# Load order of keys, queries and values, and two FFN matmuls moved ahead of a granule's transposes, in a one-core attention and FFN kernel

## The chip, the cores and the metric

The kernel runs on one core of one Trainium2 chip. The metric is device time in microseconds (us); a smaller time is better. Times inside a profile count from the start of its span, which is about 1.7 us shorter than the device time.

## The reference

Windowed attention with eight global keys feeds a feed-forward network (FFN) with a squared ReLU. There are 4 batches, 8 heads, 768 positions and a head size of 64; the FFN is 512 to 2048 to 512.

```
scores = q @ k.T / sqrt(D) - slope[h] * dist        # only global keys and the last 96 positions are kept
a      = softmax(scores)
x      = (a @ v), heads side by side                # 3072 x 512
out    = (s * relu(x @ w_in)**2 + b) @ w_out        # 3072 x 512
```

## The kernel before

The sequence is worked in twelve *granules* of 256 rows, numbered 0 to 11 in the code. The text below says third granule for `j == 2`, fifth for `j == 4`, and so on. A granule has two *blocks* of 128 rows. From the third granule on, the keys, queries and values of a granule come as six loads of 128 KB (counted as written), all issued by GpSimd (the first two granules are loaded by other lines of the code):

```
def load_granule(j):
    b, g = divmod(j, NGR)
    t = nat_tile(j)
    for i in range(GB):                  # two blocks
        sb = g * GB + i
        for n in range(2):               # keys, then queries
            nc.gpsimd.dma_start(t[:, n, i, :, :], rows_of(srcs[n], b, sb))
        nc.gpsimd.dma_start(vbuf[b % 2][:, sb, :, 0:D], rows_of(v, b, sb))
```

Keys and queries must be transposed before the scores. For the first four granules TensorE (PE) does it, through PSUM; from the fifth on it is done by DMA transposes that SyncE issues:

```
def qk_wide(j, n, evac):                 # PE: 8 transposes, then one evacuation
    ps = ps_h.tile([P, GB, HP, P], BF16, name="ps_t", tag="psh")
    for i in range(GB):
        for hp in range(HP):
            nc.tensor.transpose(ps[:, i, hp, :], nat[j][:, n, i, 2*hp : 2*hp+2, :], ident_bf[:])
    evac(qk_of(b, n)[:, g * GB : (g + 1) * GB], ps[:])

def qk_by_dma(j):                        # SyncE: key, query of block 0, then of block 1
    for i in range(GB):
        for n in range(2):
            nc.sync.dma_start_transpose(qk_of(b, n)[:, g * GB + i], ...)
```

The main body is a hand-made schedule. With cuts:

```
    load_granule(2)
    load_granule(3)
    ...
    load_granule(4)
    load_granule(5)
    ...
    p2_mm(0, 1, lo, FC)                  # second FFN product of the first granule
    p2_hold(0, 1)                        # ScalarE empties its PSUM buffer

    qk_wide(2, 0, nc.vector.tensor_copy) # third granule: keys
    qk_wide(2, 1, nc.scalar.copy)        #                queries
    make_koff(2)                         # shifted keys, VectorE
    make_voff(2)                         # shifted values, VectorE
    p2_mm(1, 0, 0, FC // 2)              # 8 matmuls of 128x512
    e8, m8, e9, m9 = scores(4)           # first scores of the third granule
    ...
    qk_by_dma(4)                         # fifth granule: keys and queries, by DMA
    ...
    finish_granule(3)
    run(scores(8))                       # first scores of the fifth granule
    make_voff(4)
    p2_mm(2, 0, 0, FC // 2)
```

## Time and profile before

| | before |
|---|---|
| device time, median of 3 runs | 209.34 us (209.31 to 209.69) |
| span in the profile | 207.7 us |
| PE busy | 97% of the span |
| third granule: transposes start, first scores start | 38.12, 41.70 us |
| fifth granule: first scores start, FFN matmuls behind them start | 60.02, 60.72 us |

The page of the kernel before, its first lines and its chain by line. The chain is followed back from the last instruction, and a share is that of the span.

```profile
span 207.7 us, 5321 instructions
PE 202.2 (97%) x2191; PEld 160.2 (77%) x2191; DVE 159.5 (77%) x336; ACT 128.7 (62%) x200; POOL 70.4 (34%) x90
...
PE 82%; DMA 15%; ACT 1%; DVE 1%; issue 0%; POOL 0%
```

PE is the limit for most of the span: it is hardly ever idle, and the chain is PE for 82% of it. The place where the chain is a DMA comes from the chain of waits in order of time (start, duration, what):

```profile
13.33 13.78 DMA w_out_bf<-in_moe_w_out_dram
27.11 0.28 issue
27.39 12.21 DMA nat<-in_q_dram
39.60 0.05 issue
39.65 0.40 PE ps_t L350 x4
40.04 1.73 PE ps L666 x8
```

The load of the third granule's second query block lands at 39.60 us, and PE waits for it. PE's own timeline there (start, duration, engine, line, operation, output and inputs, shapes, count, and in brackets the idle time before and what ended it) shows the same hole from the other side:

```profile
38.12 0.39 PE L350 MATMUL ps_t<-ident_bf,nat 128*128 128x128 bf16 x4
38.84 0.62 PE L350 MATMUL ps_t<-ident_bf,nat 128*128 128x128 bf16 x8 [0.34 <-DMA nat<-in_k_dram]
39.65 0.40 PE L350 MATMUL ps_t<-ident_bf,nat 128*128 128x128 bf16 x4 [0.18 <-DMA nat<-in_q_dram]
39.88 1.89 PE L666 MATMUL ps<-w_out_bf,gT 128*128 128x512 bf16 x8
41.70 0.40 PE L440 MATMUL ps_s<-qx,kx 64*128 64x128 bf16 x8
```

Sixteen transposes stand in three pieces with waits between. The FFN matmuls behind them needed nothing that was late, but stood behind the waiting transposes in program order.

These are the first scores of the fifth granule, in the same timeline:

```profile
60.02 0.55 PE L440 MATMUL ps_s<-qx,kx 64*128 64x128 bf16 x8
60.38 0.40 PE L440 MATMUL ps_s<-qx,ko 64*128 64x128 bf16 x8
60.72 1.04 PE L666 MATMUL ps<-w_out_bf,gT 128*128 128x512 bf16 x4
```

The same eight score matmuls take 0.40 us at 41.70 us and 0.55 us here. No wait is named, because the idle time is hidden inside the merged line. The single records of the trace show where it is: the first two of these matmuls start at 60.02 us, the third at 60.22 us. The first two need block 0 of the granule, the third needs block 1. It is a wait of about 0.15 us for something that had only just arrived, and the result turns on it.

### The profile page before, as it was taken

The page shows a single profiled execution, that of the slowest core. Times are in us where ns is not written, and L with a number is a line of the kernel's source. Part 1 is how long each engine was busy: PE and PEld are TensorE (multiplying, and loading weights), DVE is VectorE, ACT ScalarE, POOL GpSimd, SP SyncE. Part 2 cuts the span into 40 slices and gives each one's busy share as a digit, 9 for nine tenths or more (in the row PEclk, how much of TensorE's full clock was granted, in tenths as well). Part 3 has the DMA queues.
Part 4 walks back from the last instruction along what each step waited for, and adds up shares of the span by engine and source line. Part 5 has one row for each costly group of instructions (what it writes and reads, how often), then busy time and mean ns, then how long its engine had stood idle before and what let it go on. Part 6 is the DMA issues. An engine that isn't in the chain of part 4 may idle for free.

```text
span 207.7 us, 5321 instructions
## 1 busy us (share of the span) xinstructions
PE 202.2 (97%) x2191; PEld 160.2 (77%) x2191; DVE 159.5 (77%) x336; ACT 128.7 (62%) x200; POOL 70.4 (34%) x90
## 2 busy tenths in 40 slices
PE   7999999899999999999999999999999999999993
PEld 2678884456876685778888898888898889888883
DVE  7586599858989955799799974699865696737974
ACT  4975669485975648786564495664695764476200
POOL 8995334899726202805501906400000000000000
PEclk9999999999999999999999999999999999999999
DMA  5999999999999999999999999995460300240006
GB/s 162 173 179 202 207 207 177 155 152 136 116 149 135 155 156 197 147 234 205 143 230 140 113 124 201 183 204 69 52 205 3 88 17 0 53 153 0 0 7 198
DMA packets 110836, 28.17 MB, mean 136 GB/s; under 512 B 97852, under 2 KB 109308, under 8 KB 110812
## 3 DMA queue, kind: packets, MB, share of 16 engines
q0 software_dynamic: 76000, 13.11, 87.8%
q1 hardware_dynamic: 33612, 14.13, 36.8%
q10 hardware_dynamic: 1200, 0.59, 1.1%
q8 instruction: 17, 0.28, 0.6%
q14 instruction: 7, 0.06, 0.1%
HBM read 27.26 MB, written 6.29 MB: 162 GB/s over the span
## 4 chain that ended last, share of the span: by engine, by line
PE 82%; DMA 15%; ACT 1%; DVE 1%; issue 0%; POOL 0%
PE ps L618 34%; PE ps L818 24%; PE ps L666 10%; DMA w_out_bf<-in_moe_w_out_dram 7%; DMA nat<-in_q_dram 6%; PE ps_s L440 6%; PE ps_av L494 5%; DMA first<-in_q_dram 2%; PE ps_t L350 1%; ACT qx L330 1%; PE ps_last L818 0%; PE ps_x L590 0%; ACT open_bf L231 0%; ACT nat L259 0%; PE ps_t L340 0%
## 5 line engine op out<-in xcount | busy, mean ns | idle before, releaser
L618 PE MATMUL ps<-xT,w_in_bf 128*128 128x256 bf16 x768 | 90.3, 273 | 0.0
L628 ACT ACTIVATE gT<-ps 128x512 bf16<-128x512 f32 x96 | 55.8, 598 | 46.8 <-PE ps L618 46.5
L618 PEld LDWEIGHTS <-w_in_bf 128*128 128x128 bf16 x768 | 73.0, 98 | 9.4 <-DVE xT L593 0.2
L449 ACT ACTIVATE pt<-ps_s 128x1024 bf16<-128x1024 f32 (+1 forms) x44 | 39.3, 945 | 3.2 <-PE ps_s L440 3.2
L666 PE MATMUL ps<-w_out_bf,gT 128*128 128x512 bf16 x128 | 29.7, 380 | 0.0
L456 DVE TENSOR_TENSOR pt<-pt,tmpl 128x1024 bf16<-128x1024 bf16 (+1 forms) x40 | 24.6, 646 | 4.6 <-ACT pt L449 4.5
L818 PEld LDWEIGHTS <-gsum 128*128 128x128 bf16 x256 | 24.1, 98 | 3.7 <-DVE gsum L781 0.5
L792 DVE TENSOR_TENSOR gT<-gT 128x1024 bf16<-128x1024 bf16 x20 | 13.7, 687 | 11.7 <-ACT gT L628 11.7
L666 PEld LDWEIGHTS <-gT 128*128 128x128 bf16 x128 | 11.7, 98 | 13.0
L465 DVE TENSOR_TENSOR xn<-ps_av,rc 128x256 bf16<-128x256 f32 x48 | 20.4, 425 | 1.7
L818 PEld LDWEIGHTS <-gT 128*128 128x128 bf16 x200 | 18.6, 98 | 2.3
L116 POOL DMA_DIRECT2D nat<-in_k_dram x20 | 18.1, 903 | 6.2 <-issue 1.8
L116 POOL DMA_DIRECT2D nat<-in_q_dram x20 | 18.0, 902 | 5.9 <-DMA w_out_bf<-in_moe_w_out_dram 3.4
L117 POOL DMA_DIRECT2D vb<-in_v_dram x20 | 18.0, 900 | 5.9 <-DMA w_in_bf<-in_moe_w_in_dram 2.0
L464 DVE RECIPROCAL rc<-ps_av 128x4 f32<-128x4 f32 x48 | 8.6, 179 | 12.2 <-PE ps_av L494 10.3
L494 PEld LDWEIGHTS <-pt 128*128 128x128 bf16 x320 | 14.4, 97 | 2.7 <-DVE xn L465 0.7
L631 DVE TENSOR_TENSOR gT<-gT 128x512 bf16<-128x512 bf16 x32 | 13.0, 422 | 3.7 <-ACT gT L628 3.3
L122 POOL COPY gate<-xT 1x1 bf16<-1x1 bf16 x6 | 1.9, 323 | 41.0 <-DMA xT<-xn 38.9
L494 PE MATMUL ps_av<-vb,pt 128*128 128x65 bf16 x208 | 15.4, 193 | 0.0
L818 PE MATMUL ps<-w_out_bf,gsum 128*128 128x256 bf16 x128 | 15.3, 273 | 0.0
L818 PE MATMUL ps<-wsub,gsum 128*128 128x256 bf16 x128 | 15.1, 273 | 0.0
L818 PE MATMUL ps<-w_out_bf,gT 128*128 128x256 bf16 x120 | 13.9, 273 | 0.0
(112 smaller groups left out, 223.7 us busy)
## 6 DMA issues: line engine op xcount, KB each, us to landing
out_dram<-o_q SPq DMA_DIRECT2D x15, 256.0 KB, 2.5
vb<-in_v_dram POOLq DMA_DIRECT2D x24, 128.0 KB, 7.3
nat<-in_k_dram POOLq DMA_DIRECT2D x22, 128.0 KB, 6.8
nat<-in_q_dram POOLq DMA_DIRECT2D x22, 128.0 KB, 7.0
w_out_bf<-in_moe_w_out_dram POOLq DMA_DIRECT2D x4, 512.0 KB, 16.2
w_in_bf<-in_moe_w_in_dram POOLq DMA_DIRECT2D x4, 256.0 KB, 7.4
w_in_bf<-in_moe_w_in_dram POOLq DMA_DIRECT2D x2, 512.0 KB, 11.3
out_dram<-o_sb SPq DMA_DIRECT2D x4, 256.0 KB, 5.9
```

What stands on the lines that cost most here:

```text
L116: nc.gpsimd.dma_start(t[:, n, i, :, :], rows_of(srcs[n], b, sb))
L117: nc.gpsimd.dma_start(vbuf[b % 2][:, sb, :, 0:D], rows_of(v, b, sb))
L449: nc.scalar.activation(pt[:, :, 0:ncol], ps[:, :, 0:ncol], ACT.Exp, scale=QSCALE)
L456: nc.vector.tensor_tensor(pv, pv, m.rearrange("p h a c -> p h (a c)"), ALU.mult)
L465: nc.vector.tensor_tensor(dst, av[:, :, :, 0:D], rc[:].to_broadcast((P, 2, 2, D)), ALU.mult)
L494: nc.tensor.matmul(av[:, i, hi, 0 : D + 1], lhsT=pt[:, hi, c * P : (c + 1) * P], rhs=vv, start=(n == 0), stop=(n == len(terms) - 1),)
L618: nc.tensor.matmul(ps[:, i, :], lhsT=w_in_bf[:, kc, fc * P : (fc + 1) * P], rhs=xT[j][:, kc, :], start=(kc == 0), stop=(kc == KC - 1),)
L628: nc.scalar.activation(gs, ps[:], ACT.Relu)
L631: nc.vector.tensor_tensor(gs, gs, gs, ALU.mult)
L666: nc.tensor.matmul(po[:], lhsT=g_of(j)[:, fc, tb * P : (tb + 1) * P], rhs=w_out_bf[:, fc, :], start=(fc == 0), stop=(fc == FC - 1),)
L792: outs.append(lambda: nc.vector.tensor_tensor(gs, gs, gs, ALU.mult))
L818: nc.tensor.matmul(ps[:, tb, cs], lhsT=stat[:, fc, tb * P : (tb + 1) * P], rhs=mov[:, fc, cs], start=(fc == 0), stop=(fc == NH - 1),)
```

## The change

Its intent is to close the hole at the third granule, in two ways. Keys and queries of both blocks are loaded ahead of both value blocks, in every granule from the third on, so the second query block lands one load sooner. Two FFN matmuls that are ready go in front of the transposes, so PE has work while the last loads land.

```
@@ load_granule
             for n in range(2):
                 nc.gpsimd.dma_start(t[:, n, i, :, :], rows_of(srcs[n], b, sb))
-            nc.gpsimd.dma_start(vbuf[b % 2][:, sb, :, 0:D], rows_of(v, b, sb))
+        load_v(j)

@@ main body
+    p2_mm(1, 0, 0, 2)
     qk_wide(2, 0, nc.vector.tensor_copy)
     qk_wide(2, 1, nc.scalar.copy)
     make_koff(2)
     make_voff(2)
-    p2_mm(1, 0, 0, FC // 2)
+    p2_mm(1, 0, 2, FC // 2)
```

More of the change, by code (lines that the diff above doesn't have):

```diff
@@ L116, in load_granule @@
                 nc.gpsimd.dma_start(t[:, n, i, :, :], rows_of(srcs[n], b, sb))
-            nc.gpsimd.dma_start(vbuf[b % 2][:, sb, :, 0:D], rows_of(v, b, sb))
+        load_v(j)
     def hold_loads(ap):
@@ L1088 @@
     p2_hold(0, 1)
+    p2_mm(1, 0, 0, 2)
     qk_wide(2, 0, nc.vector.tensor_copy)
@@ L1094 @@
     make_voff(2)
-    p2_mm(1, 0, 0, FC // 2)
+    p2_mm(1, 0, 2, FC // 2)
     e8, m8, e9, m9 = scores(4)
```

## The prediction

> **What bounds the kernel now.** TensorE. The page gives PE 97% busy at full granted clock. The chain of waits, in order of time, is nothing but matmuls from 39.6 us to 203 us, so what makes PE get there earlier shortens the whole as much, unless another wait opens. The chain before it is a DMA stretch: from 13.3 us it follows the second-FFN weights, then the load of the third granule's queries, issued at 27.39 us and landing 12.21 us later, at 39.60 us. The timeline of PE shows the hole: the third granule's 16 transposes start at 38.12 us, the second key block's wait (0.34 us idle), the last query block's wait (0.18 us idle) and the FFN matmuls behind them start at 40.04 us. Elsewhere in the chain eight such transposes take 0.45 us, so sixteen 0.90; here they take 1.92. The hole is worth about 1.0 us.
>
> **What the change does.** It adds and removes no work.
>
> 1. Load order. The packets of the load queue in the trace show it streaming back to back, about 0.86 us for each 128 KB load. Estimated landings before: k0 36.2, q0 37.0, v0 37.85, k1 38.75, q1 39.6, v1 40.45 us. Moving v0 behind q1 puts k1 near 37.9 and q1 near 38.7; v0 goes to 39.6; v1 stays.
> 2. Two FFN matmuls (0.43 us; eight take 1.73) go in front of the transposes. They are ready at 38.12 us. The Trainium skill, "TensorE: Matmul & The Clock Gate", Part 2, says that matmuls stay in program order and only weight loads are pulled ahead; the trace agrees, since ready FFN matmuls sat behind the waiting transposes until 40.04 us. They also cover a second wait: in the changed kernel the query transposes use the PSUM buffer that ScalarE empties at 38.91 us.
>
> Estimated order after: two matmuls 38.12 to 38.55, key transposes to 39.0, query transposes to 39.45, six matmuls to 40.75, then the scores, which began at 41.70 us before. That is about 1.0 us sooner.
>
> **What could take some back.** Six matmuls instead of eight now cover the evacuations. Query copy on ScalarE: 1.01 us from about 39.65, done near 40.7, needed at 40.75. Key copy and shifted-key copies on VectorE: 1.74 us from about 39.2, done near 40.95, needed at 41.0. Both just fit; I allow 0 to 0.2 us of new waits. The shifted values need v0 at about 40.5 us, and it is there at 39.6. The first value product of this granule moves to 43.7 us, with v1 landed at 40.45. Later granules load well ahead of use.
>
> **Predicted time.** 209.34 minus about 0.95 = 208.4 us, range 208.0 to 209.0. Chances: faster by over 2%: 0.01; within 2%: 0.98; slower by over 2%: 0.01.
>
> **What would show it right or wrong.** Right: in PE's timeline no idle time at the third granule's transposes; the 16 of them in about 0.9 us; the scores of that granule beginning near 40.75 us; all later pieces of the chain shifted by 0.9 to 1.0 us. Load step wrong: the transposes still wait for a DMA. Matmul step wrong: the two matmuls wait for ScalarE. Give-back: scores waiting for the query copy on ScalarE or the shifted-key copy on VectorE.
>
> **What would make it wrong.** The weights landing later in the changed run, moving everything; a new wait of the scores larger than 0.2 us; a later place where PE waits for a fixed DMA time, so that the lead is lost again; the masks being held behind the value copy on VectorE.

## The result, and the profile after

| | before | after |
|---|---|---|
| device time, median of 4 runs each | 209.51 us (209.31 to 209.69) | 209.27 us (209.03 to 209.31) |
| ratio, 95% interval | | 0.9986 (0.9969 to 1.0004) |
| span in the profile | 207.7 us | 207.3 us |
| third granule: first scores start | 41.70 us | 40.89 us |
| fifth granule: first scores start | 60.02 us | 59.20 us |
| fifth granule: FFN matmuls behind them start | 60.72 us | 60.31 us |

A ratio is the mean time of one kernel's runs over that of the other's of the same rounds, so it is not quite the ratio of the medians quoted. The gain is 0.24 us by the medians, 0.1% of the time, and the interval of the ratio includes no gain at all. About 0.95 us was predicted.

PE's timeline after the change, at the third granule:

```profile
38.60 1.06 PE L350 MATMUL ps_t<-ident_bf,nat 128*128 128x128 bf16 x16
39.49 1.46 PE L666 MATMUL ps<-w_out_bf,gT 128*128 128x512 bf16 x5
40.89 0.40 PE L440 MATMUL ps_s<-qx,kx 64*128 64x128 bf16 x8
```

The hole is closed: the sixteen transposes are one piece with no wait, and the scores start 0.81 us sooner (41.70 to 40.89). (Five FFN matmuls are recorded where the program has six; some matmul records are missing from a trace.) The same timeline at the fifth granule:

```profile
58.66 0.61 PE L590 MATMUL ps_x<-ident_bf,xn 128*128 128x128 bf16 x8
59.20 0.23 PE L440 MATMUL ps_s<-qx,kx 64*128 64x128 bf16 x2
59.81 0.34 PE L440 MATMUL ps_s<-qx,kx 64*128 64x128 bf16 x6 [0.39 <-DMA qx<-nat]
59.98 0.40 PE L440 MATMUL ps_s<-qx,ko 64*128 64x128 bf16 x8
60.31 1.47 PE L666 MATMUL ps<-w_out_bf,gT 128*128 128x512 bf16 x5
```

PE brings the lead undiminished for 18 us: it reaches these scores at 59.20 us and not at 60.02. Two matmuls run, and then it waits, for the DMA transpose of the queries. Past the scores the lead is 0.41 us (60.72 to 60.31). The page's chain by engine has moved accordingly, with less PE and more DMA in it:

```profile
span 207.3 us, 5315 instructions
...
PE 69%; DMA 19%; POOL 6%; SPq 2%; issue 1%; DVE 0%; POOLq 0%
```

and the chain of waits in order of time now runs through this DMA:

```profile
52.10 7.67 DMA qx<-nat
59.77 0.04 issue
59.81 0.57 PE ps_s L440 x14
```

SyncE's timeline shows the four DMA transposes of the fifth granule in the kernel before:

```profile
46.85 1.31 SPq L359 DMA_TRANSPOSE kx<-nat  x1
51.02 1.75 SPq L359 DMA_TRANSPOSE qx<-nat  x1
```

and after (first and fourth only, in both):

```profile
47.08 1.29 SPq L359 DMA_TRANSPOSE kx<-nat  x1
52.10 1.27 SPq L359 DMA_TRANSPOSE qx<-nat  x1
```

The first of them is issued when the fifth granule's first keys have landed, and PE's lead does not make that sooner: 46.85 us before, 47.08 us after. The packet records of the trace (each transpose moves 512 packets of 256 bytes on SyncE's queue) give the last data packet of the fourth transpose: 59.49 us before, 59.08 us after. PE goes on 0.7 us after that packet, at 60.22 us before and 59.81 us after (up to 1.0 us in the runs below), so a last packet that comes a little ahead of PE's arrival still makes it wait. Both kernels run into the same landing there, the kernel before by about 0.15 us and the changed one by 0.39 us.

### The profile page after: what moved, and what is told of

Same layout as the page of the kernel before. It is cut to its first block, busy times and chain, and to the rows that moved or that the text cites. A ratio compares the mean times of both kernels' runs of the same rounds, so it can differ in the third digit from the quotient of the medians. Undisturbed runs are those within 1.5% of the kernel's fastest.

```text
span 207.3 us, 5315 instructions
## 1 busy us (share of the span) xinstructions
PE 201.4 (97%) x2183; PEld 160.2 (77%) x2191; DVE 159.8 (77%) x336; ACT 128.7 (62%) x200; POOL 69.3 (33%) x90
## 4 chain that ended last, share of the span: by engine, by line
PE 69%; DMA 19%; POOL 6%; SPq 2%; issue 1%; DVE 0%; POOLq 0%
PE ps L618 31%; PE ps L818 24%; DMA w_out_bf<-in_moe_w_out_dram 8%; PE ps L666 7%; PE ps_s L440 4%; DMA vb<-in_v_dram 4%; DMA qx<-nat 4%; PE ps_av L494 4%; DMA nat<-in_k_dram 3%; SPq L359 2%; POOL vb L108 2%; POOL nat L102 2%; POOL nat L116 1%; POOL w_in_bf L140 1%; PE ps_last L818 0%
## 5 line engine op out<-in xcount | busy, mean ns | idle before, releaser
L666 PE MATMUL ps<-w_out_bf,gT 128*128 128x512 bf16 x120 | 28.7, 380 | 0.5 <-issue 0.2
L108 POOL DMA_DIRECT2D vb<-in_v_dram x24 | 21.4, 905 | 7.8 <-DMA w_out_bf<-in_moe_w_out_dram 3.4
L122 POOL COPY gate<-xT 1x1 bf16<-1x1 bf16 x6 | 1.1, 176 | 40.4 <-DMA xT<-xn 38.0
```

The source lines that it names most:

```text
L666: nc.tensor.matmul(po[:], lhsT=g_of(j)[:, fc, tb * P : (tb + 1) * P], rhs=w_out_bf[:, fc, :], start=(fc == 0), stop=(fc == FC - 1),)
```

## The experiments

The theory: two limits stand in series. One is the hole at the third granule. The other is the landing of the fifth granule's DMA-transposed queries near 60 us, which PE does not set. The change removes the first, and its lead is given back at the second. The rivals: A, nothing is lost later and the gain was over-sized; B, the new load order itself delays the fifth granule; D, raised later, an early load alone makes the gain.

The table gathers what the runs showed. "Arrives" is the first score matmul of the fifth granule, "last packet" the last data packet of its fourth DMA transpose, "leaves" the start of the FFN matmuls behind these scores, all in us from the profile. The last column works from the ratio, as (ratio - 1) times the median of before in the same rounds. That median was 209.30 us in one set of rounds and 209.69 us in another on the same chip, so times of different rounds are not to be compared directly.

| run | arrives | last packet | PE's named wait | leaves | median | before | gain by ratio |
|---|---|---|---|---|---|---|---|
| before | 60.02 | 59.49 | none | 60.72 | 209.51 | | |
| after | 59.20 | 59.08 | 0.39 | 60.31 | 209.27 | 209.51 | -0.29 |
| e1 loads only | 59.43 | 59.85 | 0.90 | 61.06 | 209.69 | 209.51 | -0.13 |
| e2 matmuls only | 59.53 | 59.31 | 0.39 | 60.66 | 209.16 | 209.51 | -0.31 |
| e3 both, fifth early | 59.13 | 57.59 | none | 59.69 | 208.58 | 209.51 | -0.98 |
| e4 both, fill | 60.21 | 59.85 | none | 61.04 | 209.16 | 209.51 | -0.40 |
| e5 neither, fifth early | 60.05 | 57.99 | none | 60.60 | 209.29 | 209.30 | -0.06 |
| e6 matmuls, fifth early | 59.59 | 57.68 | none | 60.22 | 209.03 | 209.30 | -0.31 |
| e7 loads, fifth early | 59.50 | 57.72 | none | 60.06 | 208.66 | 209.30 | -0.75 |
| e8 both, sixth held | 59.23 | 56.42 | none | 59.78 | 208.77 | 209.30 | -0.54 |
| e9 both, again | 59.27 | 59.87 | 1.39 | 61.39 | 209.67 | 209.69 | +0.13 |
| e10 both, fifth early, again | 59.22 | 57.75 | none | 59.87 | 208.69 | 209.69 | -0.88 |
| e11 the same and a fill | 59.60 | 57.93 | none | 60.15 | 209.16 | 209.69 | -0.57 |

In e4 two of the FFN matmuls stand in front of the scores, so its "arrives" and "leaves" are not those of the others.

The profiles also show that little else counts in these executions. One granule later, at the start of the FFN matmuls behind the sixth granule's first scores (near 70 us), the lead or lag against the kernel before is the difference in the whole span to within 0.05 us in ten of the twelve profiles (after: 0.40 and 0.39 us ahead; e1: 0.34 and 0.34 behind; e7: 0.66 and 0.67 ahead; e9: 0.67 and 0.63 behind). The two others lose something later: e3 0.11 us and e11 0.42 us.

### Each part of the change alone (e1, e2)

The first keeps the change's load order and puts the two matmuls back:

```
-    p2_mm(1, 0, 0, 2)
     qk_wide(2, 0, nc.vector.tensor_copy)
...
-    p2_mm(1, 0, 2, FC // 2)
+    p2_mm(1, 0, 0, FC // 2)
```

> Only the load order of the change; the two FFN matmuls stay where they were. Theory (the lead made at the third granule, 38 to 41 us, is given back at the first scores of the fifth granule, near 59.8 us, because the DMA transposes of its queries land at a time that PE does not set): lead of about 0.5 us over the kernel before at the third granule's first scores, and 0.3 to 0.4 us left after the fifth granule's first scores; time about 0.3 us under before, the same as the full change. Rival A (nothing is lost later, the gain was over-sized): the same lead at 41 us and at 61 us, and a time under before by just that lead. Rival B (the new load order delays the fifth granule's loads and causes the loss): the loss is here in full, so the same times as the theory.

The second is the opposite: the kernel before, with the two matmuls moved and the load order left alone.

> Only the two FFN matmuls ahead of the third granule's transposes; load order as before. Theory: lead of about 0.4 us at the third granule's first scores; the transposes of the fifth granule's queries land where they did before (PE held until about 60.2 us), so at most 0.2 us is left after those scores, and the time is 0 to 0.2 us under before. Rival B (the load order causes the loss): the 0.4 us lead is kept to the end, time 0.4 us under before. Rival A: also 0.4 us kept.

Both parts do what they should at the third granule. Its first scores start at 41.12 us with the loads alone and at 41.22 us with the matmuls alone, leads of 0.58 and 0.48 us. Both lose at the fifth granule. PE's timeline of e1 there:

```profile
59.43 0.23 PE L440 MATMUL ps_s<-qx,kx 64*128 64x128 bf16 x2
60.56 0.34 PE L440 MATMUL ps_s<-qx,kx 64*128 64x128 bf16 x6 [0.90 <-DMA qx<-nat]
60.73 0.40 PE L440 MATMUL ps_s<-qx,ko 64*128 64x128 bf16 x8
61.06 0.82 PE L666 MATMUL ps<-w_out_bf,gT 128*128 128x512 bf16 x2
```

In this execution e1 comes out 0.34 us *behind* the kernel before (61.06 against 60.72), although it arrived 0.59 us ahead. PE's timeline of e2 has the same wait:

```profile
60.16 0.34 PE L440 MATMUL ps_s<-qx,kx 64*128 64x128 bf16 x6 [0.39 <-DMA qx<-nat]
```

In e2 a lead of 0.49 us on arrival shrinks to 0.06 us, and e2 has the old load order. So the loss does not need the new order, which tells against B as the whole cause, and A is wrong too. B as a part of it is not excluded. The two profiles with the old order and the landing left alone have the last packet at 59.49 us (before) and 59.31 us (e2); the four with the new order have it at 59.08 (after), 59.85 (e1), 59.85 (e4) and 59.87 us (e9). Three of those four are some 0.4 us later, and the fourth is the earliest of all; six profiles are too few to say more. The times themselves (0.9994 with an interval of 0.9973 to 1.0014, and 0.9985 with 0.9969 to 1.0001) cannot tell theory from rival here. Two expectations were off: e1 kept no lead at all in its profile, and e2's time came out 0.31 us under before where 0.2 at most was expected. The runs of e1 spread from 208.65 to 209.85 us, which pointed at a landing that moves from run to run (the runs of before on that chip spread as widely, from 209.19 to 210.03 us).

### The fifth granule's loads earlier (e3), and the wait filled (e4)

If the landing is the limit, moving it must free the lead. In e3 the fifth granule's keys and queries are loaded ahead of the fourth's values, which PE first reads at about 54 us:

```
     load_granule(2)
-    load_granule(3)
+    load_qk(3, 0)
+    load_qk(3, 1)
...
-    load_granule(4)
+    load_qk(4, 0)
+    load_qk(4, 1)
+    load_v(3)
+    load_v(4)
     load_granule(5)
```

> The full change, and the four key and query loads of the fifth granule put ahead of the two value loads of the fourth, so each of them lands about 1.7 us sooner. Theory: the fifth granule's DMA transposes are issued from about 45.3 us instead of 47.1 and land at least 1 us sooner; PE no longer waits at its first scores (0.39 us before), the lead of 0.8 us at 41 us is kept past 61 us, and with the small wait that the kernel before had there also gone the time is 0.8 to 1.0 us under before, 0.5 to 0.7 us under the full change. Rival A: no change against the full change, about 0.25 us under before.

PE's timeline of e3 at the fifth granule (the edit adds a line to the file, so line numbers are one higher):

```profile
59.13 0.40 PE L441 MATMUL ps_s<-qx,kx 64*128 64x128 bf16 x8
59.37 0.39 PE L441 MATMUL ps_s<-qx,ko 64*128 64x128 bf16 x8
59.69 1.90 PE L667 MATMUL ps<-w_out_bf,gT 128*128 128x512 bf16 x7
```

The wait is gone, the scores run in 0.40 us again, and PE leaves 1.03 us ahead of the kernel before. The first DMA transpose is issued at 45.02 us and the last packet comes at 57.59 us, 1.5 us sooner than after the change. The time is 208.58 us, ratio 0.9953 (0.9939 to 0.9966), a gain of 0.98 us. All five runs lie within 208.51 to 208.64 us, where the eleven runs of before on that chip spread from 209.19 to 210.03 us.

In e4 the landing is left alone and the wait is filled, with two ready FFN matmuls in front of the scores:

```
     finish_granule(3)
+    p2_mm(2, 0, 0, 2)
     run(scores(8))
     make_voff(4)
-    p2_mm(2, 0, 0, FC // 2)
+    p2_mm(2, 0, 2, FC // 2)
```

> The full change, and two FFN matmuls of the third granule (0.43 us) moved from behind the fifth granule's first scores to in front of them, the change's own trick used at the second wait. Theory: they fill the 0.39 us wait; PE leaves those scores and the remaining FFN matmuls about 0.4 us sooner than in the full change, and the time is about 0.4 us under the full change, 0.6 to 0.7 us under before. Rival A (no wait there that counts): the move changes nothing, same time as the full change within 0.1 us.

The time was 0.40 us under before by ratio (0.9981, 0.9968 to 0.9994), less than the 0.6 to 0.7 expected. PE's timeline of e4 shows why this execution cannot be set against the profile of after:

```profile
59.69 0.38 PE L666 MATMUL ps<-w_out_bf,gT 128*128 128x512 bf16 x1 [0.24 <-ACT gT L628]
60.21 0.67 PE L440 MATMUL ps_s<-qx,kx 64*128 64x128 bf16 x8
60.70 0.40 PE L440 MATMUL ps_s<-qx,ko 64*128 64x128 bf16 x8
```

The filling matmuls had a wait of their own (0.24 us, on ScalarE), and the last packet came at 59.85 us, 0.77 us later than in the profile of after, so the scores still took 0.67 us. e1, on the same chip with the same last packet, had a time 0.53 us longer. In the two profiles PE goes on after the landing at nearly the same time (60.54 us in e4, 60.56 us in e1) and e4's span is 0.44 us shorter, which is close to the 0.43 us of the two matmuls. That fits a fill that works; one execution of each does not show it.

### The early loads without the change, or with half of it (e5, e6, e7)

These separate the two limits. Each is an earlier kernel with e3's edit: the kernel before (e5), the matmuls alone (e6), the load order alone (e7).

> The kernel before with only the fifth granule's key and query loads put ahead of the fourth granule's values; neither part of the change. Theory (two limits in series: the hole at the third granule, then the landing of the fifth granule's transposed queries near 60 us): the hole of 1.0 us at 38 to 40 us stays, so only the small wait at the fifth granule's first scores (about 0.15 us in the trace of before) goes; time 0.1 to 0.3 us under before, and a narrower spread of the runs, since that landing varies from run to run. Rival D (the early load alone made the gain of 0.9 us, the change nothing): time about 0.9 us under before.

> The two FFN matmuls in front, without the change's load order, with the fifth granule's early loads. Theory: the lead of about 0.48 us that the matmuls alone made at the third granule's first scores is now kept, plus about 0.15 us at the fifth granule; time 0.5 to 0.75 us under before. Rival D: about 0.9 us under before, as with both parts.

> The change's load order without the two matmuls, with the fifth granule's early loads. Theory: the lead of about 0.58 us that the load order alone made at the third granule's first scores is now kept, plus about 0.15 us at the fifth granule; time 0.6 to 0.85 us under before, with no wait for the fifth granule's queries. Rival D: about 0.9 us.

e5 settles rival D: the early loads alone gain 0.06 us (ratio 0.9997, 0.9984 to 1.0009). That is under the 0.1 to 0.3 us expected, with an interval that includes part of it. In its profile the small wait at the fifth granule is gone, and the hole at the third stays. e7 gains 0.75 us (0.9964, 0.9951 to 0.9976), as expected: 0.58 us from the third granule and the small wait. PE's timelines of e5 and of e7 at the fifth granule, where the scores take 0.40 us in both:

```profile
60.05 0.40 PE L441 MATMUL ps_s<-qx,kx 64*128 64x128 bf16 x8
```

```profile
59.50 0.40 PE L441 MATMUL ps_s<-qx,kx 64*128 64x128 bf16 x8
```

So the same load order measured 0.13 us with the second limit in place (e1, not clear of noise) and 0.75 us without it.

e6 missed. It kept its lead past the fifth granule in the profile (60.22 against 60.72, so 0.50 us), but the time was only 0.31 us under before. Its profiled execution took 210.56 us and has a new wait, of the same kind, at the sixth granule. PE's timeline of e6:

```profile
70.50 0.34 PE L441 MATMUL ps_s<-qx,kx 64*128 64x128 bf16 x6 [1.42 <-DMA qx<-nat]
```

e6 and e5 keep the old order within the sixth granule, so its second keys and queries come one load later. The old order is not needed for a wait there: e10 below has the new order and meets one too. Whether a smaller wait there took the rest in e6's other runs is not shown.

### Fewer loads beside the transposes (e8)

Why does the landing come so late, 12 us after the first issue? The Trainium skill, "DMA: Bandwidth & Descriptors", section "Queues, rings and completion order", says that each DMA engine goes round the queues for which it has work, so transposes and loads share the engines. e8 tests whether this sharing costs time here. In it the sixth granule's loads are held until about 50.4 us, and the next two granules' until the fourth has finished:

```
-    load_granule(5)
...
-    finish_granule(2)
+    x_by_pe(2)
+    hold_loads(xT[2][0:1, 0, GT - 1 : GT])
+    load_granule(5)
...
-    finish_granule(3)
+    x_by_pe(3)
+    hold_loads(xT[3][0:1, 0, GT - 1 : GT])
+    load_granule(6)
+    load_granule(7)
```

> The full change, with the loads of the sixth granule held back until the third granule's FFN input has been transposed (about 51 us), and those of the seventh and eighth until the fourth's; the load order up to the fifth granule is the change's. If the fifth granule's transposes land late because the sixth granule's loads share the DMA engines with them, they have the engines to themselves from about 50 to 54 us and the last lands at least 1 us sooner than 59.8 us; no wait of PE at its first scores, time 0.8 to 1.0 us under before. If their pace is their own (issue and queue), the last still lands near 59.8 us and the time is that of the full change, 0.3 us under before.

The first issue is where it was (46.90 us), and the last packet comes at 56.42 us, 2.7 us sooner than after the change. The third transpose, with no packet of a load beside it, took 0.81 us from its first packet to its last (51.83 to 52.64); with loads beside it the same transpose took 1.86 us after the change (55.79 to 57.65). PE does not wait:

```profile
59.23 0.40 PE L440 MATMUL ps_s<-qx,kx 64*128 64x128 bf16 x8
59.46 0.39 PE L440 MATMUL ps_s<-qx,ko 64*128 64x128 bf16 x8
59.78 1.90 PE L666 MATMUL ps<-w_out_bf,gT 128*128 128x512 bf16 x8
```

So a second, unlike way to move the landing frees the lead as well, and sharing with the sixth granule's loads is part of why it is late; here the runs agree with the page. The gain was 0.54 us (0.9974, 0.9959 to 0.9989), under the 0.8 expected: one run took 209.50 us where the others lay between 208.58 and 208.91. What held that one is not known.

### Once more on one chip (e9, e10, e11)

The full change, the version with early loads, and that version with one more fill, to check the theory's word on the spread and to look for a better kernel. The edit of e11 moves two FFN matmuls in front of the next place where e3's PE waited for a DMA (0.17 us at 83.30 us):

```
-        p2_mm(j, tb, FC // 2, FC)
+        p2_mm(j, tb, FC // 2 + 2 * tb, FC)
...
-        [lambda: p2_mm(3, 1, 0, FC // 2), u1(4, 0)],
+        [lambda: p2_mm(3, 1, 0, FC // 2 + 2), u1(4, 0)],
```

> The full change once more, unaltered, on one chip with the next two. Theory: its time follows the landing of the fifth granule's transposed queries, so PE waits there again, 0.2 to 0.9 us in the profile, the lead left after those scores is 0 to 0.5 us and the runs spread over 0.3 us or more; time 0.1 to 0.45 us under before.

> The full change with the fifth granule's early loads, once more, on the same chip. Theory: no wait at the fifth granule's first scores; time 0.8 to 1.05 us under before, 0.5 us or more under the full change, runs within 0.3 us.

> The same, and two FFN matmuls of the fourth granule moved in front of the fifth granule's first FFN matmuls, where the profile of the version before showed the next wait of PE on a DMA (0.17 us, for the transposed attention output). If that wait is steady they fill it: no wait there, time 0.1 to 0.2 us under the version without them, 1.0 to 1.2 us under before. If it is there in some runs only, no difference within 0.1 us.

The very same changed kernel gained nothing here: 209.67 us against 209.69, ratio 1.0006 (0.9992 to 1.0020). PE's timeline of e9:

```profile
59.27 0.23 PE L440 MATMUL ps_s<-qx,kx 64*128 64x128 bf16 x2
60.89 0.34 PE L440 MATMUL ps_s<-qx,kx 64*128 64x128 bf16 x6 [1.39 <-DMA qx<-nat]
61.39 0.39 PE L666 MATMUL ps<-w_out_bf,gT 128*128 128x512 bf16 x1
```

PE arrives 0.75 us ahead of the kernel before and leaves 0.67 us behind it. The last packet came at 59.87 us, 0.79 us later than in the first profile of the same program, so the landing does move from one execution to the next. The gain was expected to be 0.1 to 0.45 us and the wait at most 0.9 us, so this run was worse than the theory's numbers, by its own mechanism. e10, on the same chip, repeats e3: 208.69 us, ratio 0.9958 (0.9944 to 0.9972). Its runs were expected within 0.3 us and spread over 0.50 us, from 208.58 to 209.08 us. The slowest is the profiled one, and PE's timeline of it shows the next limit of the same kind, at the sixth granule:

```profile
68.50 0.23 PE L441 MATMUL ps_s<-qx,kx 64*128 64x128 bf16 x2
69.06 0.34 PE L441 MATMUL ps_s<-qx,kx 64*128 64x128 bf16 x6 [0.33 <-DMA qx<-nat]
```

Past the fifth granule's scores it is 0.85 us ahead of the kernel before, past the sixth's 0.34 us, and its span is 0.36 us shorter. e3's profile has no wait there (its eight scores take 0.40 us at 68.31 us).

e11 failed. The wait it aimed at is gone, but e10's profile has no wait there either, without the fill, so e11 does not test the fill. Its time (209.16 us, ratio 0.9973) is longer than e10's, outside what was expected. In its profile PE reached the third granule's transposes 0.37 us later than in e10 (39.00 against 38.63), before any edited instruction, and it has a new wait of 0.30 us on VectorE at 100.52 us. How much of this the edit causes is open. e3's version stays the best that was run.

## Why the prediction was wrong

The predicted time, 208.4 us with a range from 208.0 to 209.0, missed 209.27 us. Point by point:

- *PE is the limit, and the hole at the third granule is real.* Right. The waits are gone after the change.
- *The load order and the two matmuls close it.* Right. Alone they made leads of 0.58 and 0.48 us at the third granule, together 0.81 us. They overlap, since they fill the same hole.
- *Matmuls keep program order* (the Trainium skill, "TensorE: Matmul & The Clock Gate", Part 2). The profiles agree: at 59.20 us in the changed kernel the FFN matmuls again stood behind scores that waited.
- *The size of the lead, about 1.0 us.* Slightly too large. The FFN matmuls' start before was taken from the chain (40.04 us), the rest from the timeline, where the same matmuls start at 39.88 us. Read from one view, the lead is 0.39 us at that point plus 0.43 us for the two matmuls already done, 0.82 us, which is what was measured.
- *New waits of up to 0.2 us on the evacuations.* None of size was seen: the scores began 1.40 us after the start of the six FFN matmuls, and before 1.82 us after the start of eight.
- *"Later granules load well ahead of use."* **This is the step that failed.** Their loads do land early, but from the fifth granule on the use is not PE's: four DMA transposes come in between, issued from 47 us and landing just short of 60 us. The kernel before met that landing with 0.15 us of wait. There was no slack behind the hole, so the 0.81 us lead was cut to 0.41 us in one execution, and in another (e9) to less than nothing. The prediction did list "a later place where PE waits for a fixed DMA time" among the dangers, but gave it no weight.

That the landing is the cause is shown by e3, e7, e8 and e10, which move it and keep the lead past it, and by e5, which moves it without the change and gains nothing clear. Still open are why the landing moves by 0.8 us between executions of one program, whether the new load order has a part in that, and the smaller gains of e6 and e8 (the profile of e8 lost 0.14 us of its lead at the sixth granule).

## What to carry to other kernels

When PE is the limit for the whole chain, a wait closed early is worth its size only if every later wait on a DMA has more slack than that: list the later DMA landings and measure the slack of each before counting a gain. A wait can hide in a merged line of the timeline, so compare the duration of the same group at two places, here 0.40 and 0.55 us. Two limits in series have to be removed together: apart they gained 0.29 us at best and 0.06 us, together 0.98 us, and 0.88 us when repeated. Behind them stands the next one: in the profiles of e6 and e10 PE waited for the sixth granule's queries.

## What the Trainium skill lacked or had wrong

- "DMA: Bandwidth & Descriptors" has rates for DMA transposes, but no trn2 time for one from SBUF to SBUF with loads beside it. Here the four transposes of the fifth granule, of 128x512 bf16 each, needed 6.0 to 7.9 us from issue to last packet in the changed kernel, and 2.1 to 4.5 us in e8 with the loads held back.
- The same page, section "Anatomy of one DMA — SWDGE (gpsimd) path", fits one load as 2.0 us plus its bytes over 436 GB/s, which gives 2.3 us for 128 KB (an estimate from that page). In the full queue of this kernel the median from issue to landing was 7.3 us for the value loads, and loads followed each other at 0.86 us. The fit is for one transfer, and these stood in a queue, so it is not shown wrong; the page lacks the time in a full queue.
- No page says how far such landings move between executions of one program: here the last packet came at 59.08 us in one and at 59.87 us in another.
